# Two query tiles, four result buffers and moved weight splits in a linear-attention and expert kernel

## Chip, cores and metric

The kernel runs on one core of a Trainium2 chip. The metric is the device time of one execution in microseconds (us); three executions of the kernel before gave a median of 298.92 us (298.61 to 301.04).

## The reference

Linear attention with random features over 4 batches, 8 heads, 576 positions (2304 rows of 512 in all), then a top-1 mixture of 8 experts with a capacity per expert.

```python
proj = einsum('bhsd,md->bhsm', x * scale, omega)          # phi: 128 features per head
h = proj - sum(x*x)/2;  phi = exp(h - max(h)) / sqrt(m)   # the max and the square cancel per row
kv = einsum('bhsm,bhsd->bhmd', k_p, v);  z = sum(k_p, axis=2)
x = einsum('bhsm,bhmd->bhsd', q_p, kv) / (einsum('bhsm,bhm->bhs', q_p, z) + 1e-6)
logits = x @ w_gate;  expert_idx = argmax(logits);  gate_w = softmax(logits)[expert_idx]
# per expert, the first `capacity` rows in order are kept
y = relu(x_e @ w1[e]) @ w2[e];  out[i] = gate_w[i] * y[...]   # dropped rows are zero
```

## The kernel before

Every instruction is recorded in the order in which the Python code runs; each engine works through its own list in that order and waits on semaphores. So the order of the code sets the order of the work. Generators in a list `tasks` are advanced by `step(n)` at fixed points of the loops, and `pause(n)` in such a generator lets n of these points pass: that is how side work is spread between the main steps.

The work has three stages, each with its own pool of PSUM banks (`stage(name, pairs, singles)`; a pair is two banks).

- **Key stage** (`psk`: two sum banks, three pairs). Loop `n` over 18 groups of four (batch, head pair, row tile) units: `project` (TensorE, `pjk`), `maxima` (VectorE, `mxk`), `exponent` (ScalarE, eight activations, `exk`), and two groups later the key sums `kv_acc` (TensorE, `ksum`). When half a batch is summed, `kv_out` copies the sums (`kv_sb`, VectorE), GpSimd copies them to `kvc`, TensorE transposes them (`ktr`), VectorE copies (`kvT`), TensorE multiplies by the gate weights (`ksm`), VectorE copies the product into `kv_sb`.
- **Query stage** (`psq`: two pairs, two single banks, two banks `qsum`). Loop `t` over 18 tiles of 128 rows: project tile t (`pjq`), sums of tile t-3 (`numer`, `qsum`), maxima of tile t (`mxq`), results of tile t-3 (`normalise`: `den`, `rec`, `xr`, `lg`, and the write-out to `x_d` on SyncE), transposes of tile t-2 (`transposed`: `qtr`, copies `qpT` on ScalarE), exponentials of tile t (`exq`). The results tile `xr` rotates over three buffers. Side tasks: `route` for three groups of tiles (0 to 4, 5 to 11, 12 to 17) finds each row's expert and its rank and scatters it to a table (GpSimd); `first_item` finds the expert of row 0, loads its weights and splits them in a high and a low part on GpSimd (`split_w_hi`, `split_w_lo`: `w1hi`, `w1lo`, `w2hi`); `first_rows` reads the first item's rows from the table and gathers them (`xg`). Behind the last tiles `transpose_x` transposes the gathered rows and splits them (`xtri`, `xhi` on ScalarE, `xlo` on VectorE).
- **Item stage** (`psi`: four `h` banks, two `y`, two others). Items of 576 rows of one expert: `mm1` makes 16 half steps (8 features blocks f, two halves of rows) of 12 matmuls each (`hi`), `mm2` the second product. In item 0 the last group's rank product (`posr`) and the list of items (`items_list`, `cps`) stand behind the first two half steps. Three items run.

A tile of a new pool waits until the old pool has been read to the end. The rest of the order follows from the functions that the change touches:

## Time and profile before

| | us |
|---|---|
| median of three runs | 298.92 |
| the profiled execution, as timed | 299.85 |
| its span, first to last instruction | 298.1 |
| TensorE busy | 276.0 |
| ScalarE busy | 159.0 |
| VectorE busy | 147.8 |
| GpSimd busy | 79.2 |
| mean granted TensorE clock, share of full speed | 0.983 |

The busy time of TensorE counts matmuls that overlap; what can be gained is where it stands idle, and where its clock is low. The key stage runs to about 50 us, the query stage to 123 us, item 0 to 179 us, items 1 and 2 to 282 us, and then the last results are written.

### The profile page before, as it was taken

How to read it: one execution, taken by the hardware profiler on the slowest of the kernel's cores; microseconds unless marked ns; L12 is line 12 of the kernel's file. 1: busy time of each engine (PE TensorE's matmuls, PEld its weight loads, DVE VectorE, ACT ScalarE, POOL GpSimd, SP SyncE). 2: the span in 40 equal slices, each digit the busy share in tenths (PEclk: the TensorE clock that was granted, in tenths of full speed). 3: DMA queues.
4: the chain of work that ended last, by engine and by line, in shares of the span. 5: the costliest groups of instructions: out<-in, count | busy, mean ns of one | idle time of the engine just before them, and what ended most of it. 6: DMA issues, size and time to landing. Idle time of an engine off the chain costs nothing.

```text
span 298.1 us, 7419 instructions
## 1 busy us (share of the span) xinstructions
PE 276.0 (93%) x2971; PEld 240.0 (81%) x2971; DVE 147.8 (50%) x295; ACT 159.0 (53%) x458; POOL 79.2 (27%) x92
## 2 busy tenths in 40 slices
PE   7999999799999878799999999999999999999940
PEld 5899998688888766799958879996888999778830
DVE  2566664587986796666522332543342152532410
ACT  2998885799899877222243324443531435334210
POOL 1010011003659777035052111700121171011210
PEclk9999999999999999899999999999999999999995
DMA  6998940237991986504869103921811196062120
GB/s 196 388 378 299 318 168 2 55 128 254 373 370 37 360 292 179 178 3 118 274 185 306 38 35 98 315 67 5 297 57 51 37 335 106 0 235 104 43 71 2
DMA packets 30959, 50.37 MB, mean 169 GB/s; under 512 B 5587, under 2 KB 18387, under 8 KB 30900
## 3 DMA queue, kind: packets, MB, share of 16 engines
q1 hardware_dynamic: 27620, 41.46, 41.1%
q0 software_dynamic: 3152, 8.28, 9.2%
q8 instruction: 25, 0.41, 0.6%
q14 instruction: 18, 0.15, 0.2%
q10 hardware_dynamic: 144, 0.07, 0.1%
HBM read 36.80 MB, written 13.28 MB: 168 GB/s over the span
## 4 chain that ended last, share of the span: by engine, by line
PE 73%; DVE 6%; DMA 5%; issue 5%; POOL 4%; SPq 2%; ACT 2%; POOLq 0%; DVEq 0%; ACTq 0%
PE hi L662 9%; PE hi L664 9%; PE hi L663 9%; PE yi L678 7%; PE yi L680 7%; PE yi L679 7%; PE ksum L200 6%; PE pjk L137 5%; PE yi L688 4%; PE qsum L469 3%; PE xtri L323 3%; DMA kraw<-kT 2%; PE pjq L137 2%; PE qtr L460 2%; POOL w1lo L125 2%
## 5 line engine op out<-in xcount | busy, mean ns | idle before, releaser
L662 PE MATMUL hi<-xhi,w1hi 128*128 128x288 f32 x192 | 57.7, 300 | 1.7 <-DVE mxr L349 1.7
L664 PE MATMUL hi<-xlo,w1hi 128*128 128x288 f32 x192 | 57.3, 299 | 0.0
L663 PE MATMUL hi<-xhi,w1lo 128*128 128x288 f32 x192 | 57.2, 298 | 0.0
L667 ACT ACTIVATE hhii<-hi 128x288 fp32r<-128x288 f32 (+1 forms) x48 | 18.5, 385 | 50.0 <-PE hi L664 50.0
L152 ACT ACTIVATE exk<-pjk,mxk 128x128 f32<-128x128 f32 x144 | 38.7, 409 | 8.2 <-DVE mxk L144 8.2
L152 ACT ACTIVATE exq<-pjq,mxq 128x128 f32<-128x128 f32 x144 | 39.5, 403 | 4.8 <-DVE mxq L144 4.8
L670 DVE SCALAR_TENSOR_TENSOR hloi<-hi,hhii 128x288 fp32r<-128x288 f32 (+1 forms) x48 | 20.1, 423 | 39.2 <-ACT hfi L669 27.0
L106 POOL DMA_INDIRECT out<-ysi,idx x15 | 14.6, 975 | 93.9 <-ACT ysi L705 78.3
L678 PE MATMUL yi<-w2hi,hhii 128*128 128x512 f32 x96 | 38.8, 404 | 0.0
L662 PEld LDWEIGHTS hi<-xhi,w1hi 128*128 128x128 f32 x192 | 36.7, 191 | 2.2 <-issue 1.8
L327 DVE TENSOR_TENSOR xlo<-xtri,xhi 128x512 fp32r<-128x512 f32 (+1 forms) x20 | 12.4, 635 | 51.6 <-ACT xhi L326 51.6
L680 PE MATMUL yi<-w2lo,hhii 128*128 128x512 f32 x96 | 37.9, 395 | 0.0
L679 PE MATMUL yi<-w2hi,hloi 128*128 128x512 f32 x96 | 37.9, 395 | 0.0
L663 PEld LDWEIGHTS hi<-xhi,w1lo 128*128 128x128 f32 x192 | 36.7, 191 | 0.0
L664 PEld LDWEIGHTS hi<-xlo,w1hi 128*128 128x128 f32 x192 | 36.6, 191 | 0.0
L705 ACT ACTIVATE ysi<-yi,idx 128x512 f32<-128x512 f32 x12 | 8.3, 688 | 45.9 <-issue 39.2
L144 DVE TENSOR_REDUCE mxk<-pjk 128x8 f32<-128x1024 f32 x18 | 21.9, 1224 | 16.4 <-PE pjk L137 12.1
L311 POOL DMA_INDIRECT xg<-x_d,idx x20 | 22.2, 1110 | 25.5 <-DMA idx<-tab_d 11.7
L469 PE MATMUL qsum<-kv_sb,qpT 128*64 128x73 f32 x576 | 22.4, 229 | 4.3 <-DVE xr L485 3.0
L144 DVE TENSOR_REDUCE mxq<-pjq 128x8 f32<-128x1024 f32 x18 | 21.9, 1216 | 7.8 <-PE pjq L137 7.8
L469 PEld LDWEIGHTS qsum<-kv_sb,qpT 128*64 128x64 f32 x576 | 19.9, 136 | 6.8 <-issue 4.2
L106 POOL DMA_INDIRECT tab_d<-pay,slot x18 | 18.7, 1037 | 22.1 <-DVE ilcnt L592 11.6
(105 smaller groups left out, 425.8 us busy)
## 6 DMA issues: line engine op xcount, KB each, us to landing
w1raw<-w SPq DMA_DIRECT2D x16, 512.0 KB, 7.0
w2raw<-w SPq DMA_DIRECT2D x16, 512.0 KB, 6.4
qraw<-qT SPq DMA_DIRECT2D x6, 768.0 KB, 8.7
x_d<-xr SPq DMA_DIRECT2D x18, 256.0 KB, 5.4
out<-zero_sb SPq DMA_DIRECT2D x6, 768.0 KB, 8.5
v<-va SPq DMA_DIRECT2D x7, 650.0 KB, 7.8
kraw<-kT SPq DMA_DIRECT2D x6, 576.0 KB, 8.5
kraw<-kT SPq DMA_DIRECT2D x3, 192.0 KB, 3.4
```

The costliest lines, as they stand in the source:

```text
L106: ins = nc.gpsimd.indirect_dma_start(out=dst, out_offset=bass.IndirectOffsetOnAxis(ap=index, axis=0), in_=src, in_offset=None, bounds_chec ...
L137: nc.tensor.matmul(pj[:, i, s * M : (s + 1) * M], raw[r, :], om_sb[r, :], start=True, stop=True, skip_group_check=True)
L144: nc.vector.tensor_reduce(mx, pj, op=ALU.max, axis=AX.X, negate=True)
L152: nc.scalar.activation(ex[:, i, s, :], pj[:, i, s, :], AF.Exp, bias=mx[:, i, s : s + 1], scale=1.0)
L311: nc.gpsimd.indirect_dma_start(out=big["xg"][0:n, i, :], out_offset=None, in_=x_d[0:rows, :], in_offset=bass.IndirectOffsetOnAxis(ap=big[" ...
L469: nc.tensor.matmul(qsum[c : c + 64, h // 4, o : o + ROW], qpT[:, h, c : c + 64], kv_sb[(t * 128 + c) // S][:, h, :], start=(h % 4 == 0), s ...
L662: nc.tensor.matmul(pt, whi_[:, k, fs], xhi[:, k, sl], start=(k == 0), stop=False)
L663: nc.tensor.matmul(pt, wlo_[:, k, fs], xhi[:, k, sl], start=False, stop=False)
L664: nc.tensor.matmul(pt, whi_[:, k, fs], xlo[:, k, sl], start=False, stop=(k == 3))
L678: nc.tensor.matmul(pt, hhi[:, f, sl], w2hi, start=(f == 0), stop=False)
L679: nc.tensor.matmul(pt, hlo[:, f, sl], w2hi, start=False, stop=False)
L680: nc.tensor.matmul(pt, hhi[:, f, sl], w2lo, start=False, stop=(f == 7))
```

## The change

The diff without the lines that only follow from it:

```diff
@@ -40,4 +40,4 @@
 
-HI_AT = ({}, {0: ((2, 0),), 1: ((2, 1),), 3: ((2, 2),), 4: ((2, 3),)})
-LO_AT = ({f + 2: ((2, f),) for f in range(4)}, {1: ((2, 0),), 2: ((2, 1),), 5: ((2, 2),), 6: ((2, 3),)})
+HI_AT = ({0: ((2, 0),), 1: ((2, 1),), 3: ((2, 2),), 4: ((2, 3),)}, {0: ((2, 0),), 1: ((2, 1),), 3: ((2, 2),), 4: ((2, 3),)})
+LO_AT = ({2: ((2, 0),), 3: ((2, 1),), 5: ((2, 2),), 6: ((2, 3),)}, {1: ((2, 0),), 2: ((2, 1),), 5: ((2, 2),), 6: ((2, 3),)})
 
@@ -208,4 +208,7 @@
 
-    kvc = const.tile([128, 4 * M], F32, name="kvc")
-    kvT = const.tile([128, 4 * M], F32, name="kvT")
+
+    def row_buffer(name):
+        return small.tile([128, ROW, H], F32, tag="xr", name=name, bufs=4)
+
+    kv_bufs = {}
 
@@ -213,2 +216,5 @@
         yield
+        if g == 0:
+            kv_bufs[b] = row_buffer(f"kvc{b}").rearrange("p c h -> p (c h)")
+        kvc = kv_bufs[b]
         kv = kv_sb[b][:, 4 * g : 4 * g + 4, :]
@@ -223,2 +229,3 @@
             nc.tensor.transpose(tr[:, i * M : (i + 1) * M], kvc[:, i * M : (i + 1) * M], id_sb)
+        kvT = row_buffer(f"kvT{b}").rearrange("p c h -> p (c h)")[:, 0 : 4 * M]
         nc.vector.tensor_copy(kvT, tr)
@@ -329,3 +336,3 @@
 
-    head = {"quiet": True}
+    head = {"routed": 0}
     place = {"ranks": False}
@@ -346,17 +353,4 @@
         sel, p, base, drop, sm = tl(t3, "s"), tl([128, T], "p"), tl([128, T], "b"), tl([128, T], "o"), tl([128, T], "m")
-        head["quiet"] = a == 0
+        gap = 2 if 0 < a and z < NT else 1
         yield from pause(2)
...
         if a == 0:
@@ -366,2 +360,16 @@
             count(bas, a)
+            yield
+        nc.vector.tensor_reduce(mx, lg[:, a:z, :], op=ALU.max, axis=AX.X)
+        yield from pause(gap)
...
@@ -392,14 +400,14 @@
         nc.vector.tensor_reduce(p, sel, op=ALU.add, axis=AX.X)
-        yield
+        yield from pause(gap)
...
         for t in range(a, z):
@@ -407,3 +415,3 @@
             yield from pause(2 if 0 < a and z < NT else 0)
-        head["quiet"] = False
+        head["routed"] += 1
         if z == T0:
@@ -434,13 +442,12 @@
             load_w(2, c, ev)
-
-            while c > 1 and head["quiet"]:
+            yield from pause(2)
+        for c in range(4):
+
+            while head["routed"] < (0, 1, 1, 2)[c]:
                 yield
             split_w_hi(1, c, nc.gpsimd)
-            yield from pause(3 if c < 2 else 1)
+            yield from pause(1 if c else 3)
             for k in range(4):
                 split_w_lo(1, c, nc.gpsimd, k)
-                yield from pause(2 if c < 2 else 1)
-        for c in range(4):
-            split_w_hi(2, c, nc.gpsimd)
-            yield from pause(4)
+                yield from pause(1 if c else 2)
 
@@ -478,3 +485,3 @@
     def normalise(t):
-        xr = small.tile([128, ROW, H], F32, tag="xr", name=f"xr{t}", bufs=3)
+        xr = row_buffer(f"xr{t}")
         av = qsum[:, :, 0 : 4 * ROW].rearrange("p b (h c) -> p c b h", c=ROW)
@@ -501,3 +508,9 @@
     LK = 2
-    ex_l = {}
+    ex_l, exq, qpT_l = {}, {}, {}
+
+    def project_tile(t):
+        c, o = t // QT, t % QT * 128
+        return project([qc[c][:, p, o : o + 128] for p in range(NP)], f"q{t}")
+
+
     for n in range(NK + LK):
@@ -519,2 +532,4 @@
             pj = project_keys()
+        elif n >= NK:
+            pj = project_tile(n - NK)
         step()
@@ -526,2 +541,4 @@
                     load_k(k1 // 2, k1 % 2)
+        else:
+            exq[n - NK] = exponent(pj, maxima(pj, f"q{n - NK}"), f"q{n - NK}")
         step(2)
@@ -529,4 +546,4 @@
             tasks.append(setup())
-        if n in (NK - 4, NK - 2):
-            load_q(0 if n == NK - 4 else 1)
+        if n in (NK - 5, NK - 3):
+            load_q(0 if n == NK - 5 else 1)
     kstack.close()
@@ -539,8 +556,8 @@
 
-    exq, qpT_l = {}, {}
-    for t in range(NT + 3):
+    for t in range(LK, NT + 3):
         if t < NT:
-            c, o = t // QT, t % QT * 128
-            pj = project([qc[c][:, p, o : o + 128] for p in range(NP)], f"q{t}")
-            if t % QT == 0 and c + 2 < NT // QT:
+            pj = project_tile(t)
+        if t == LK or (t < NT and t % QT == 0):
+            c = t // QT
+            if c + 2 < NT // QT:
                 load_q(c + 2)
@@ -567,9 +584,6 @@
             exq[t] = exponent(pj, mx, f"q{t}")
-        else:
-            for i in range(2 * (t - NT), min(2 * (t - NT) + 2, NSUB)):
-                transpose_x(i, "i0")
+        for i in {NT - 1: (0,), NT: (1, 2), NT + 1: (3, 4)}.get(t, ()):
+            transpose_x(i, "i0")
         step(3)
     qstack.close()
-    qps.close()
-    ctx.enter_context(stage("i", 0, 2))
 
@@ -740,4 +754,4 @@
 
-                for _ in chain(*tasks):
-                    pass
+                while tasks:
+                    step()
                 ro = route(*GROUPS[NT - 1])
@@ -749,3 +763,4 @@
                 for half in range(2):
-                    hp = bank(f"h{nm}{f}{half}", "h", 4)
+
+                    hp = pair(f"h{half}")[:, 0, :] if j + f == 0 else bank(f"h{nm}{f}{half}", "h", 4)
                     mm1(f, half, hp, hhi, hlo, hf)
@@ -754,2 +769,4 @@
                 if j == 0 and f == 0:
+                    qps.close()
+                    ctx.enter_context(stage("i", 0, 2))
                     for _ in chain(ro, items_list()):
```

Place by place:

- Key stage: tiles 0 and 1 of the queries are projected in the two extra turns of the key loop (n = 18 and 19), ahead of `ksm` of batch 2 and behind the last key sums, in pairs of the key stage's pool. The query loop starts at t = 2. The first two query loads are issued one turn earlier.
- `xr` has four buffers, and `kvc` and `kvT` use the same four.
- `route` of the middle group takes twice as many points; the count of earlier rows stands at its start.
- `first_item` loads all of w2 first; the w1 splits on GpSimd go on at three places: block 0 at once, 1 and 2 behind the first group's scatters, 3 behind the second's. The high parts of w2 are made on ScalarE in item 0.
- The transposes of the gathered rows start one tile earlier (one, two, two).
- The first two half steps of item 0 use pairs of the query stage; the item stage's pool is opened behind them.

TensorE's list where the key stage passes into the query stage; `ksum` are key sums, `pjq0` the projection of query tile 0, `qtr` transposes, `qsum` the sums of a tile. Before:

```order
L200 MATMUL ksum1_108<-v31_581,exk16_777 64x130 x4
L229 MATMUL ksm2_848<-wg_sb_73,kvT_95 64x16 x8
L200 MATMUL ksum1_108<-v31_581,exk17_815 64x65 x16
L137 MATMUL pjq0_913<-om_sb_67,qraw0_710 128x128 x8
L223 MATMUL ktr3_936<-id_sb_72,kvc_94 128x128 x4
L137 MATMUL pjq1_942<-om_sb_67,qraw0_710 128x128 x8
L229 MATMUL ksm3_951<-wg_sb_73,kvT_95 64x16 x8
L137 MATMUL pjq2_972<-om_sb_67,qraw0_710 128x128 x8
L460 MATMUL qtr00_984<-id_sb_72,exq0_927 128x128 x4
L460 MATMUL qtr02_990<-id_sb_72,exq0_927 128x128 x4
L137 MATMUL pjq3_1005<-om_sb_67,qraw1_786 128x128 x8
L469 MATMUL qsum_912<-kv_sb0_68,qpT0_983 64x73 x16
```

There the projections of tiles 0 to 2 all stand behind the last key sums (`exk17`), with the last batch's `ktr3` and `ksm3` between them. TensorE's list at the same place now:

```order
L200 MATMUL ksum1_106<-v31_582,exk16_782 64x130 x4
L137 MATMUL pjq0_852<-om_sb_67,qraw0_676 128x128 x8
L236 MATMUL ksm2_873<-wg_sb_73,kvT2_832 64x16 x8
L200 MATMUL ksum1_106<-v31_582,exk17_818 64x65 x16
L137 MATMUL pjq1_899<-om_sb_67,qraw0_676 128x128 x8
L137 MATMUL pjq2_958<-om_sb_67,qraw0_676 128x128 x8
L467 MATMUL qtr00_973<-id_sb_72,exq0_864 128x128 x4
L467 MATMUL qtr02_979<-id_sb_72,exq0_864 128x128 x4
L229 MATMUL ktr3_994<-id_sb_72,kvc3_834 128x128 x4
L137 MATMUL pjq3_1001<-om_sb_67,qraw1_752 128x128 x8
L476 MATMUL qsum_957<-kv_sb0_68,qpT0_972 64x73 x16
L236 MATMUL ksm3_1028<-wg_sb_73,kvT3_999 64x16 x8
```

Two projections moved up between the key sums, and `ktr3` and `ksm3` of the last batch moved down behind the first transposes and the first sums.

VectorE's list around the results of tiles 11 and 12, where the routing of tiles 5 to 11 begins (`mxr5`, `dr5`, `vr5`, `vm`, `oh`, and the count `cum`). Before:

```order
L485 TENSOR_TENSOR xr11_1773<-qsum_912,rec11_1776 128x584
L489 TENSOR_REDUCE lg_81<-xr11_1773 128x8
L349 TENSOR_REDUCE mxr5_1781<-lg_81 128x7
L351 TENSOR_TENSOR dr5_1782<-lg_81,mxr5_1781 128x56
L353 SCALAR_TENSOR_TENSOR vr5_1784<-dr5_1782,desc_sb_77 128x56
L358 TENSOR_REDUCE vm_84<-vr5_1784 128x7
L360 TENSOR_TENSOR oh_82<-vr5_1784,vm_84 128x56
L144 TENSOR_REDUCE mxq15_1844<-pjq15_1816 128x8
L482 TENSOR_SCALAR den12_1847<-qsum_912 128x8
L484 RECIPROCAL rec12_1849<-den12_1847 128x8
L485 TENSOR_TENSOR xr12_1846<-qsum_912,rec12_1849 128x584
L335 TENSOR_REDUCE cum_83<-oh_82 128x8
```

There five routing steps stand in one piece ahead of the maxima of tile 15. VectorE's list at the same place now:

```order
L496 TENSOR_REDUCE lg_81<-xr11_1770 128x8
L342 TENSOR_REDUCE cum_83<-oh_82 128x8
L362 TENSOR_REDUCE mxr5_1778<-lg_81 128x7
L364 TENSOR_TENSOR dr5_1779<-lg_81,mxr5_1778 128x56
L144 TENSOR_REDUCE mxq15_1838<-pjq15_1811 128x8
L489 TENSOR_SCALAR den12_1841<-qsum_957 128x8
L491 RECIPROCAL rec12_1843<-den12_1841 128x8
L492 TENSOR_TENSOR xr12_1840<-qsum_957,rec12_1843 128x584
L366 SCALAR_TENSOR_TENSOR vr5_1781<-dr5_1779,desc_sb_77 128x56
L496 TENSOR_REDUCE lg_81<-xr12_1840 128x8
L371 TENSOR_REDUCE vm_84<-vr5_1781 128x7
L373 TENSOR_TENSOR oh_82<-vr5_1781,vm_84 128x56
```

The routing steps stood in one piece between `lg` of tile 11 and the maxima of tile 15; now the later three stand behind the results of tile 12, and the count stands ahead.

TensorE's list at the end of the query stage, behind the sums of tile 15; `xtri` are the transposes of the gathered rows. Before:

```order
L460 MATMUL qtr160_2051<-id_sb_72,exq16_1937 128x128 x4
L460 MATMUL qtr162_2057<-id_sb_72,exq16_1937 128x128 x4
L323 MATMUL xtri00_2063<-id_sb_72,xg_905 128x128 x4
L323 MATMUL xtri01_2070<-id_sb_72,xg_905 128x128 x4
L469 MATMUL qsum_912<-kv_sb3_71,qpT16_2050 64x73 x16
L460 MATMUL qtr170_2105<-id_sb_72,exq17_2004 128x128 x4
L460 MATMUL qtr172_2111<-id_sb_72,exq17_2004 128x128 x4
L323 MATMUL xtri02_2117<-id_sb_72,xg_905 128x128 x4
L323 MATMUL xtri03_2124<-id_sb_72,xg_905 128x128 x4
L469 MATMUL qsum_912<-kv_sb3_71,qpT17_2104 64x73 x16
L323 MATMUL xtri04_2155<-id_sb_72,xg_905 128x64 x4
L662 MATMUL hi000_2192<-xhi_906,w1hi0_883 128x288
```

There the last transpose of the gathered rows stands between the last tile's sums and the first half step. TensorE's list at the same place now:

```order
L476 MATMUL qsum_957<-kv_sb3_71,qpT15_1981 64x73 x16
L467 MATMUL qtr160_2046<-id_sb_72,exq16_1932 128x128 x4
L467 MATMUL qtr162_2052<-id_sb_72,exq16_1932 128x128 x4
L330 MATMUL xtri01_2058<-id_sb_72,xg_950 128x128 x4
L330 MATMUL xtri02_2065<-id_sb_72,xg_950 128x128 x4
L476 MATMUL qsum_957<-kv_sb3_71,qpT16_2045 64x73 x16
L467 MATMUL qtr170_2109<-id_sb_72,exq17_1994 128x128 x4
L467 MATMUL qtr172_2115<-id_sb_72,exq17_1994 128x128 x4
L330 MATMUL xtri03_2121<-id_sb_72,xg_950 128x128 x4
L330 MATMUL xtri04_2128<-id_sb_72,xg_950 128x64 x4
L476 MATMUL qsum_957<-kv_sb3_71,qpT17_2108 64x73 x16
L676 MATMUL h0_2190<-xhi_951,w1hi0_928 128x288
```

The transposes of the gathered rows moved one tile up, and the sums of the last tile now stand directly ahead of the first half step, which is in a bank of the query stage (`h0`).

## Rows read from the trace of the kernel before

**Rows 1.** Busy time by stretch. Columns: the stretch, its length, the busy time (and instructions) of TensorE, its weight loads, VectorE, ScalarE and GpSimd, the granted TensorE clock as a share of full speed, the DMA share and GB/s.

```profile
46.90:58.20 11.30, 8.92 (x162) 7.68 (x162) 6.29 (x10) 6.63 (x26) 0.80 (x2) 1.00 0.04 6
...
106.00:123.16 17.16, 13.84 (x235) 11.88 (x232) 12.88 (x36) 11.69 (x32) 10.03 (x11) 1.00 0.57 183
...
123.16:150.90 27.74, 27.74 (x202) 27.32 (x204) 16.58 (x57) 6.84 (x23) 8.63 (x8) 0.94 0.48 150
```

**Rows 2.** Instructions in order of time, all engines, where the key stage passes into the query stage. Columns: start, duration, engine, line, operation, output and input, shapes, count; in brackets the idle time of the engine before it and what ended it.

```profile
49.01 1.13 PE L200 MATMUL ksum<-v,exk 128*64 128x65 f32 x32
...
50.67 1.16 PE L137 MATMUL pjq<-om_sb,qraw 64*128 64x128 f32 x16 [0.53 <-DVE kv_sb L215]
...
51.77 0.66 PE L223 MATMUL ktr<-id_sb,kvc 128*128 128x128 f32 x4
...
51.94 1.22 DVE L144 TENSOR_REDUCE mxq<-pjq 128x8 f32<-128x1024 f32 x1 [1.32 <-PE pjq L137]
...
53.20 2.18 ACT L152 ACTIVATE exq<-pjq,mxq 128x128 f32<-128x128 f32 x8 [3.88 <-DVE mxq L144]
...
53.81 0.65 PE L229 MATMUL ksm<-wg_sb,kvT 128*64 128x16 f32 x16 [0.30 <-DVE kvT L224]
...
55.43 1.16 PE L137 MATMUL pjq<-om_sb,qraw 64*128 64x128 f32 x16 [0.97 <-ACT exq L152]
...
57.98 1.12 ACT L461 COPY qpT<-qtr 128x512 f32<-128x512 f32 x2
...
58.19 1.16 PE L137 MATMUL pjq<-om_sb,qraw 64*128 64x128 f32 x16 [0.58 <-ACT exq L152]
...
59.28 1.25 PE L469 MATMUL qsum<-kv_sb,qpT 128*64 128x73 f32 x32
...
59.45 1.22 DVE L144 TENSOR_REDUCE mxq<-pjq 128x8 f32<-128x1024 f32 x1 [1.60 <-PE pjq L137]
...
61.02 0.77 DVE L485 TENSOR_TENSOR xr<-qsum,rec 128x584 f32<-128x584 f32 x1
...
64.78 1.16 PE L137 MATMUL pjq<-om_sb,qraw 64*128 64x128 f32 x16
```

**Rows 3.** Instructions in order of time, TensorE, in the query stage and at the start of item 0: those ahead of which it idles.

```profile
79.77 1.25 PE L469 MATMUL qsum<-kv_sb,qpT 128*64 128x73 f32 x32 [0.66 <-DVE xr L485]
...
93.41 1.25 PE L469 MATMUL qsum<-kv_sb,qpT 128*64 128x73 f32 x32 [0.28 <-DVE xr L485]
...
101.14 1.25 PE L469 MATMUL qsum<-kv_sb,qpT 128*64 128x73 f32 x32 [1.08 <-DVE xr L485]
...
105.75 1.25 PE L469 MATMUL qsum<-kv_sb,qpT 128*64 128x73 f32 x32 [1.25 <-DVE cum L335]
...
112.53 1.25 PE L469 MATMUL qsum<-kv_sb,qpT 128*64 128x73 f32 x32 [1.01 <-DVE xr L485]
...
115.09 1.15 PE L323 MATMUL xtri<-id_sb,xg 128*128 128x128 f32 x8 [0.29 <-ACT qpT L461]
...
118.72 1.15 PE L323 MATMUL xtri<-id_sb,xg 128*128 128x128 f32 x8 [0.29 <-ACT qpT L461]
...
123.16 0.37 PE L662 MATMUL hi<-xhi,w1hi 128*128 128x288 f32 x1 [1.72 <-DVE mxr L349]
```

**Rows 4.** Instructions in order of time, VectorE: the subtraction of the three routing groups, and a results tile.

```profile
75.50 1.00 DVE L351 TENSOR_TENSOR dr<-lg,mxr 128x40 f32<-128x40 f32 x1
...
100.23 0.77 DVE L485 TENSOR_TENSOR xr<-qsum,rec 128x584 f32<-128x584 f32 x1 [1.80 <-DMA x_d<-xr]
...
101.53 1.08 DVE L351 TENSOR_TENSOR dr<-lg,mxr 128x56 f32<-128x56 f32 x1
...
123.16 0.21 DVE L351 TENSOR_TENSOR dr<-lg,mxr 128x48 f32<-128x48 f32 x1
```

**Rows 5.** Instructions in order of time, GpSimd: weight splits and scatters.

```profile
72.65 2.79 POOL L125 TENSOR_TENSOR w1lo<-w1raw,w1hi 128x256 fp32r<-128x256 f32 x4
...
75.41 1.04 POOL L122 TENSOR_SCALAR w1hi<-w1raw 128x1024 fp32r<-128x1024 f32 x1
...
101.47 1.07 POOL L122 TENSOR_SCALAR w2hi<-w2raw 128x1024 fp32r<-128x1024 f32 x1
...
111.81 1.00 POOL L106 DMA_INDIRECT tab_d<-pay,slot  x1 [0.30 <-issue]
...
113.12 0.97 POOL L106 DMA_INDIRECT tab_d<-pay,slot  x1 [0.30 <-issue]
```

**Rows 6.** Instructions in order of time, ScalarE: the exponentials of tile 17.

```profile
112.13 2.19 ACT L152 ACTIVATE exq<-pjq,mxq 128x128 f32<-128x128 f32 x8
```

**Rows 7.** Instructions in order of time, TensorE, VectorE and ScalarE, behind the first two half steps of item 0: the rank product, VectorE's read of the second half step, and the Relus of the first halves of two feature blocks that follow each other.

```profile
127.95 0.20 PE L374 MATMUL posr<-oh,tri_b 128*128 128x48 bf16 x1
...
128.65 0.39 DVE L670 SCALAR_TENSOR_TENSOR hloi<-hi,hhii 128x224 fp32r<-128x224 f32 x1 [2.18 <-ACT hfi L669]
...
130.04 0.41 ACT L667 ACTIVATE hhii<-hi 128x288 fp32r<-128x288 f32 x1 [1.43 <-PE hi L664]
...
133.23 0.41 ACT L667 ACTIVATE hhii<-hi 128x288 fp32r<-128x288 f32 x1 [1.12 <-PE hi L664]
```

**Rows 8.** Busy time by stretch as in rows 1, two stretches of 2 us at the start of item 0.

```profile
124.00:126.00 2.00, 2.00 (x12) 2.00 (x11) 0.65 (x3) 0.41 (x1) 0.00 (x0) 0.57 1.03 384
126.00:128.00 2.00, 2.00 (x12) 1.93 (x12) 0.46 (x1) 0.00 (x0) 0.00 (x0) 0.58 0.08 23
```

More of the change, by code (lines that the diff above doesn't have):

```diff
@@ L366, in route @@
             count(bas, a)
+            yield
+        nc.vector.tensor_reduce(mx, lg[:, a:z, :], op=ALU.max, axis=AX.X)
+        yield from pause(gap)
+        nc.vector.tensor_tensor(d, lg[:, a:z, :], mx.unsqueeze(2).to_broadcast(t3), op=ALU.subtract)
+        yield from pause(gap)
+        nc.vector.scalar_tensor_tensor(
+            val, d, 0.0, desc_sb.unsqueeze(1).to_broadcast(t3), op0=ALU.is_ge, op1=ALU.mult
+        )
+        nc.scalar.activation(ex, d, AF.Exp)
+        yield from pause(gap)
+        nc.vector.tensor_reduce(vm[:, a:z], val, op=ALU.max, axis=AX.X)
+        yield from pause(gap)
+        nc.vector.tensor_tensor(oh[:, a:z, :], val, vm[:, a:z].unsqueeze(2).to_broadcast(t3), op=ALU.is_equal)
+        yield from pause(gap)
         while not place["ranks"]:
@@ L392, in route @@
         nc.vector.tensor_reduce(p, sel, op=ALU.add, axis=AX.X)
-        yield
+        yield from pause(gap)
         nc.vector.tensor_scalar(drop, p, cap_f, BIG, op0=ALU.is_ge, op1=ALU.mult)
         nc.vector.scalar_tensor_tensor(base, vm[:, a:z], -float(REG), p, op0=ALU.mult, op1=ALU.add)
-        yield
+        yield from pause(gap)
         nc.vector.scalar_tensor_tensor(slot[:, a:z], drop, float(E * REG), base, op0=ALU.add, op1=ALU.add)
-        yield
+        yield from pause(gap)
         nc.vector.tensor_reduce(sm, ex, op=ALU.add, axis=AX.X)
-        yield
+        yield from pause(gap)
         nc.vector.tensor_scalar(sm, sm, 1e-9, None, op0=ALU.add)
-        yield
+        yield from pause(gap)
         nc.vector.reciprocal(pay[:, a:z, 1].bitcast(F32), sm)
-        yield
+        yield from pause(gap)
         for t in range(a, z):
```

12 lines of the change are left out of this document (removed).

## The prediction

> **What bounds the kernel now.** I read the stretches first, then the instructions in order of time where TensorE idles. TensorE is the bound nearly everywhere: outside the entry and the end of the query stage it idles only where a result is late. The table by stretch shows three places that the change touches [rows 1]. The entry into the query stage has TensorE busy 8.92 of 11.30 us, the end of that stage 13.84 of 17.16 us, and the first half of item 0 has no idle time but a clock of 0.94. In between, single waits of 0.66 to 1.25 us stand on TensorE's row [rows 3]. All times below are of the profiled execution (span 298.1 us, 299.85 us as timed); that is 0.9 us above the median of 298.92, and I carry the difference in us to the median.
>
> **1. The entry: two projections moved forward.** Before, the key sums end at 49.01 + 1.13 = 50.1. The projection of tile 0 starts at 50.67, its maximum at 51.94, its exponentials at 53.20, and the projection of tile 2 waits for the latter (0.97 us), that of tile 3 for the exponentials of tile 1 (0.58 us) [rows 2]. The change puts the projections of tiles 0 and 1 ahead of and behind the last key sums. This starts the chain earlier: exponentials of tile 0 from about 51.2. But these two tiles now lie in the banks of the key stage's pool, and the first tile of the query stage's pool waits for the whole old pool, as [rows 2] show: the projection at 50.67 waits 0.53 us for VectorE's last copy out of a key sum's bank, though it writes another bank. The last reader of the old pool now is the set of eight exponentials of tile 1. Step by step: last key sums end at 50.1 + 1.1 (one projection, 50.67 to 51.77) = 51.2; tile 1 projected by 52.3; its maximum from 52.5 (0.17 later, as 51.77 to 51.94) to 53.7; its exponentials, 2.18, to 56.0. Only then comes tile 2. TensorE idles 52.3 to 56.0, 3.7 us in one piece, where it had 2.4 in four pieces.
>
> From there: tile 2 projected 57.1, first transposes (about 1.0) 58.1; the transposes of the last batch's sums, which used to fill a gap, wait for the first copy of a transposed half (half of 1.12) and end at 58.9; tile 3 projected 60.0; first sums (about 1.2) 61.2; the gate product of the last batch (about 0.5) 61.7. Its copy on VectorE stands ahead of the maximum of tile 3, so this maximum starts at 62.0 instead of 60.2. From the start of a maximum to the end of the results tile takes 61.02 + 0.77 - 59.45 = 2.34, so the results are there at 64.35; TensorE, ready for the next sums at 63.8, waits 0.6. Then 1.2 + 1.0 to the projection of tile 5: 66.6. Before it is at 64.78 [rows 2]. **Cost +1.85 us.** The bounds: -1.9 (the exponentials start 2 us earlier and nothing else is in the way) to +2.3.
>
> **2. The clock at the entry.** [...] The stretch at half clock cost 1.6 us: 24 matmuls took 127.95 - 123.16 = 4.79, where the next 24 take 133.23 - 130.04 = 3.19 [rows 7]. [...] **Cost +1.3 us**, bounds 0 and 1.6. [...]
>
> **3. The body of the query stage.** Four buffers instead of three for the results: the two waits of VectorE for a buffer that is still being written out (the longer is 1.80 us at 100.23 [rows 4]) go, since the buffer of four tiles ago left one tile earlier. They stand behind TensorE's waits of 0.28 and 1.08 us. The wait of 1.25 us behind them is VectorE's lateness passed on: the late results, then a block of routing steps in one piece, one of which (the subtraction) took 1.08 us instead of 0.21 [rows 3, 4]. Both long subtractions end with a split of GpSimd that started beside them (75.41 + 1.04, 101.47 + 1.07), and the one with GpSimd idle took 0.21 [rows 4, 5]. The change takes both splits away from these places: the second w1 split waits for the first scatter, the w2 splits go to ScalarE. So the wait of 0.66 us behind the first block goes too, and spreading the second block over two tiles takes the rest. **Gain 0.66 + 0.28 + 1.08 + 1.25 = 3.27 us**; bounds 1.9 (if the 1.25 stays as 0.9 and the 0.66 only halves) and 3.3.
>
> [...]
>
> **4. The end of the stage.** Waits of 1.01, 0.29, 0.29 and 1.72 us [rows 3], 3.3 in all. The 1.72 is the new pool waiting for the last split of x; the first two half steps now use old query banks and need no new pool. But the transposes of x, drawn one tile forward, take a bank that ScalarE empties late: the copy of x behind the first transpose stands behind the eight exponentials of tile 17 (2.19), and the second half of tile 16's transposes stands behind that (copies of 0.56 each) [rows 2, 6]. By the same stepping as above this makes one wait of 1.5 us, and about 0.4 in small ones. **Gain 3.3 - 1.9 = 1.4 us**; bounds 0.7 and 2.5. The first item then starts at about 120.4.
>
> **5. Behind the first two half steps.** The pool is now opened here, so the rank product waits until VectorE has read the second half step's bank: before, the product stands at 127.95 right behind the matmuls, and that read ends at 128.65 + 0.39 [rows 7]. **Cost +1.1 us**, bounds 0.7 and 1.9 (with the collision of 3). And with the 1.72 us wait goes the half clock of [rows 8]: **gain 1.6 us**, 0 if the waits of 1.5 and 1.1 us bring it down as well.
>
> **Nothing for the rest.** Four casts of w2 (about 1 us each, as GpSimd's) join ScalarE in item 0, where it works 1.0 of every 3.19 us between Relus, with four banks of slack; without that slack, 1 us each. The last w1 split ends at about 127 and is needed at the seventh feature step, near 140; were it late, TensorE would wait by as much. SyncE issues two w2 loads earlier, ahead of two result copies, which the fourth buffer covers.
>
> **Sum.** +1.85 + 1.3 - 3.27 - 1.4 + 1.1 - 1.6 = -2.0 us: 298.92 - 2.0 = 296.9.
>
> **Rivals.**
> - The clock stays up at the entry (the drop of [rows 8] came after transposes and several waits, not after one). Then -3.3: 295.6. Chance 0.27.
> - The early projection works: tile 2 is not held for tile 1's exponentials, and the entry gains 1.9 where I lose 1.85 + 1.3. Then 291.9. Against it stands the wait at 50.67 for a bank it does not use. Chance 0.08.
> - Half clock at the end as well: the 1.5 us wait lies between 1.25 (no drop) and 1.72 (drop). Another 1.4: 298.3. Chance 0.15.
> - Slower than before: half clock at the entry does not heal within a tile, because at half clock the chain from projection to exponentials keeps TensorE waiting. A tile takes (64.78 - 58.19) / 2 = 3.3 us, 6.6 at half clock; from 0.6 of a further tile on the gain of 2.0 is eaten, with one it is 300.2, with two 303.5. For it: ScalarE is nearly as full as TensorE there. Against: the drop of [rows 8] healed by itself. Chance 0.08.
> - The forecast: 0.42.
>
> **How the numbers follow.** About 1% (3 us) is what a measurement of this kernel can tell from no change. Faster by more than that means below 295.9: the early projection (0.08), two thirds of the case with the clock up (0.18) and a quarter of the forecast's own spread (0.10) give 0.36. Slower by over 1% (above 301.9) needs two tiles at half clock or several bounds at once: 0.06. The rest, 0.58, is within 1%. The range leaves out 0.08 at the bottom and about 0.08 at the top: from 295.6 less the open bounds of the entry and the end (1.8), 293.8, to 298.3 with the collision of 0.8 and some room, 299.4.
>
> **What would show it.** Entry: one wait of about 3.7 us ahead of the third projection, put down to ScalarE's exponentials, and a lower clock around 56 to 60; its absence breaks step 1 or 2. Body: no result tile waits for its buffer, both subtractions at 0.2 us, the four waits gone. End: a wait of about 1.5 us inside tile 16's transposes; first half step at about 120.4 (plus the clock's 1.3). Item 0: a wait of about 1.1 us ahead of the rank product, put down to VectorE's read of the half step, and clock 1.00 behind it. I am wrong if the entry costs nothing, or if half clock shows in more places than the entry.

## The result and the profile after

The changed kernel takes 302.14 us (median of 20 runs; 300.56 to 304.26), the kernel before 299.68 in 20 runs beside it: ratio 1.0082, 95% interval 1.0063 to 1.0101. It is slower by 2.5 us, where 2.0 us less was forecast; the time lies outside the range. The profiled execution of the changed kernel spans 300.3 us (before 298.1) at a mean clock of 0.977 (before 0.983). Each trace is one execution: over its 20 runs the mean clock of the changed kernel goes from 0.970 to 0.982, with 0.976 in the middle; over 21 later runs the kernel before has 0.971 to 0.989, with 0.982 in the middle.

The difference by places, each from the start of the named instruction in the two traces:

| place | before | after | later by | this stretch | forecast |
|---|---|---|---|---|---|
| projection of tile 5 | 64.78 | 68.15 | +3.37 | +3.37 | +3.15 |
| projection of tile 17 | 108.15 | 108.55 | +0.40 | -2.97 | -3.27 |
| first half step | 123.16 | 122.36 | -0.80 | -1.20 | -1.4 |
| first Relu of the fourth feature block | 136.63 | 138.10 | +1.47 | +2.27 | -0.5 |
| first Relu of item 1 | 181.00 | 182.56 | +1.56 | +0.09 | 0 |
| end of the span | 298.1 | 300.3 | +2.2 | +0.6 | 0 |

The first three stretches came out nearly as worked out; the fourth has the other sign. (In the runs of the next section, but for two, every version took some 11 us more, the kernel before among them: 310.8 to 312.1 us.)

The entry, which answers to [rows 2]: the changed kernel's TensorE in order of time, idle time in brackets.

```profile
56.19 1.16 PE L137 MATMUL pjq<-om_sb,qraw 64*128 64x128 f32 x16 [3.58 <-ACT exq L152]
57.28 1.76 PE L467 MATMUL qtr<-id_sb,exq 128*128 128x128 f32 x8
59.01 1.09 PE L229 MATMUL ktr<-id_sb,kvc 128*128 128x128 f32 x4
60.03 1.59 PE L137 MATMUL pjq<-om_sb,qraw 64*128 64x128 f32 x16
...
65.95 1.25 PE L476 MATMUL qsum<-kv_sb,qpT 128*64 128x73 f32 x32 [0.62 <-DVE xr L492]
...
68.15 1.16 PE L137 MATMUL pjq<-om_sb,qraw 64*128 64x128 f32 x16
```

There is one wait of 3.58 us ahead of the third projection, put down to the exponentials. Behind it `qtr`, `ktr` and `pjq3` take up to 1.7 times as long as elsewhere: for part of this stretch the granted clock is half of full speed (0.50 from 58 to 60.5 us; the mean from 54 to 64 us is 0.83), called half clock below. In the stretches of [rows 8] the kernel before has it too: 1.00 up to 124.25, and 0.50 in each quarter of a us from 124.5 to 127.5. The rank product behind the first two half steps, which answers to [rows 7]:

```profile
128.12 0.18 PE L382 MATMUL posr<-oh,tri_b 128*128 128x48 bf16 x1 [2.32 <-DVE hloi L684]
```

VectorE and GpSimd of the changed kernel just ahead of it; the last routing group, which answers to [rows 4, 5]:

```profile
124.31 0.21 DVE L364 TENSOR_TENSOR dr<-lg,mxr 128x48 f32<-128x48 f32 x1
124.56 1.59 DVE L366 SCALAR_TENSOR_TENSOR vr<-dr,desc_sb 128x48 f32<-128x48 f32 x1
...
126.42 0.54 DVE L373 TENSOR_TENSOR oh<-vr,vm 128x48 bf16<-128x48 f32 x1
...
127.32 0.75 DVE L684 SCALAR_TENSOR_TENSOR hloi<-h,hhii 128x288 fp32r<-128x288 f32 x2
```

```profile
125.01 1.08 POOL L122 TENSOR_SCALAR w1hi<-w1raw 128x1024 fp32r<-128x1024 f32 x1
126.17 2.79 POOL L125 TENSOR_TENSOR w1lo<-w1raw,w1hi 128x256 fp32r<-128x256 f32 x4
```

The split of the fourth w1 block meets the routing group (the collision, below): two steps together take 2.13 us instead of 0.4, the read of the half step's bank (`hloi`) comes that much later, and the rank product waits 2.32 us for it instead of 1.1. Busy time by stretch in the changed kernel (columns as in [rows 8]; the clock is the third number from the end):

```profile
128.00:130.00 2.00, 1.88 (x18) 1.87 (x18) 1.42 (x10) 0.00 (x0) 0.96 (x2) 0.81 0.05 17
130.00:132.00 2.00, 2.00 (x10) 2.00 (x10) 1.72 (x16) 0.41 (x1) 1.41 (x2) 0.50 0.01 0
132.00:134.00 2.00, 2.00 (x15) 2.00 (x14) 1.76 (x11) 0.68 (x3) 1.58 (x2) 0.84 0.02 1
```

The half clock did not go with the wait that it stood behind: it moved behind the new one. The same view around the first half steps shows 1.00 until 128. The first Relu of the fourth feature block, before and after:

```profile
136.63 0.41 ACT L667 ACTIVATE hhii<-hi 128x288 fp32r<-128x288 f32 x1 [1.35 <-PE hi L664]
```

```profile
138.10 0.41 ACT L681 ACTIVATE hhii<-hi 128x288 fp32r<-128x288 f32 x1 [1.13 <-PE hi L678]
```

### The profile page after: what moved, and what is told of

It reads as the page before. It is cut to its first block, busy times and chain, and to the rows that moved or that the text cites. A ratio compares the mean times of both kernels' runs of the same rounds, so it can differ in the third digit from the quotient of the medians.

```text
span 300.3 us, 7418 instructions
## 1 busy us (share of the span) xinstructions
PE 278.3 (93%) x2971; PEld 241.8 (81%) x2971; DVE 147.7 (49%) x295; ACT 162.1 (54%) x462; POOL 73.8 (25%) x88
## 4 chain that ended last, share of the span: by engine, by line
PE 64%; DVE 5%; DMA 4%; issue 2%; ACT 2%; POOL 0%; DVEq 0%; ACTq 0%
PE hi L676 8%; PE hi L678 8%; PE hi L677 8%; PE yi L692 7%; PE yi L693 7%; PE yi L694 7%; DMA x_d<-xr 4%; PE qsum L476 4%; PE yi L702 4%; PE pjq L137 3%; PE qtr L467 3%; PE xtri L330 3%; DVE xr L492 2%; ACT exq L152 1%; DVE mxq L144 1%
## 5 line engine op out<-in xcount | busy, mean ns | idle before, releaser
L676 PE MATMUL hi<-xhi,w1hi 128*128 128x288 f32 x184 | 55.2, 300 | 0.0
L678 PE MATMUL hi<-xlo,w1hi 128*128 128x288 f32 x184 | 54.9, 299 | 0.0
L677 PE MATMUL hi<-xhi,w1lo 128*128 128x288 f32 x184 | 54.9, 299 | 0.0
L681 ACT ACTIVATE hhii<-hi 128x288 fp32r<-128x288 f32 (+1 forms) x46 | 17.7, 384 | 46.1 <-PE hi L678 46.1
L678 PEld LDWEIGHTS hi<-xlo,w1hi 128*128 128x128 f32 x184 | 35.3, 192 | 0.0
L676 PEld LDWEIGHTS hi<-xhi,w1hi 128*128 128x128 f32 x184 | 35.1, 191 | 0.1
L677 PEld LDWEIGHTS hi<-xhi,w1lo 128*128 128x128 f32 x184 | 35.2, 191 | 0.0
L468 ACT COPY qpT<-qtr 128x512 f32<-128x512 f32 x36 | 19.6, 591 | 9.9 <-PE qtr L467 6.8
L137 PE MATMUL pjq<-om_sb,qraw 64*128 64x128 f32 x288 | 21.3, 288 | 3.6 <-ACT exq L152 3.6
L200 PE MATMUL ksum<-v,exk 128*64 128x65 f32 (+1 forms) x576 | 23.4, 232 | 0.2 <-ACT exk L152 0.2
```

The lines of the kernel that those rows point to most:

```text
L137: nc.tensor.matmul(pj[:, i, s * M : (s + 1) * M], raw[r, :], om_sb[r, :], start=True, stop=True, skip_group_check=True)
L200: nc.tensor.matmul(acc[c : c + 64, i * 2 * VW + o : i * 2 * VW + o + (z - a) * VW], ex[:, i, c : c + 64], v[:, i, a * VW : z * VW], start= ...
L468: nc.scalar.copy(qpT[:, 2 * p : 2 * p + 4, :], tr.rearrange("p (h t) -> p h t", h=4))
L676: nc.tensor.matmul(pt, whi_[:, k, fs], xhi[:, k, sl], start=(k == 0), stop=False)
L677: nc.tensor.matmul(pt, wlo_[:, k, fs], xhi[:, k, sl], start=False, stop=False)
L678: nc.tensor.matmul(pt, whi_[:, k, fs], xlo[:, k, sl], start=False, stop=(k == 3))
```

## The experiments

Ratios are to the kernel before in the same group of runs.

**The changed kernel again**, as the control. 

> The changed kernel itself, beside the next three on one chip. On the chips of the runs so far the kernel before took 311 to 312 us instead of 299.7, so a ratio of a variant to it says little of its ratio to the changed kernel. If the same holds for the changed kernel, its ratio is 1.008 as measured first; if the slower chips lengthen other places in it, it is above 1.008 and their places show as waits that the first profiles don't have.

The ratio is 1.014 (1.006 to 1.022). Its row at the rank product:

```profile
142.57 0.18 PE L382 MATMUL posr<-oh,tri_b 128*128 128x48 bf16 x1 [0.99 <-DVE hloi L684]
```

```profile
142.00:144.00 2.00, 1.43 (x17) 1.43 (x17) 1.36 (x7) 1.02 (x2) 0.00 (x0) 1.00 0.02 6
144.00:146.00 2.00, 2.00 (x17) 2.00 (x16) 1.69 (x16) 0.41 (x1) 1.06 (x1) 1.00 0.00 0
```

In this trace TensorE stands still for 5.62 us while GpSimd sends the second group's scatters (such stalls are shown below for the kernel before). GpSimd has finished its split by 136.3, before the first step of the last routing group that could meet it, at 138.80; `vr` takes 0.21, the wait is 0.99, and the clock behind it stays at 1.00. So the same program without the collision has about the wait that step 5 worked out, and no half clock behind it.

**The entry.** First the early projection is undone in the changed kernel:

```diff
-        elif n >= NK:
-            pj = project_tile(n - NK)
...
-    for t in range(LK, NT + 3):
+    for t in range(NT + 3):
...
```

> The changed kernel with its first part alone undone: the projections of tiles 0 and 1 stand behind the last key sums again, and the query loads one turn later. My theory (the two early tiles hold the whole old pool, and the wait they make brings the clock down) expects what the traces show as the difference at the projection of tile 5, 68.15 against 64.78, so 3.4 us less than the changed kernel: about 298.8 us beside its 302.1, no wait over 1 us and clock 1.00 between 50 and 64 us. The rival (the loss lies behind the query stage, and the delay of the entry is taken back by waits that the body has anyway) expects under 1 us, about 301.5.

The ratio is 1.011 (1.007 to 1.015), against 1.014 for the control of another group: the intervals are too wide to tell. On its trace the projection of tile 5 starts at 64.41, no wait between 50 and 64 us is over 0.96 us and the clock is 1.00. Then the early projection alone in the kernel before, in a group where that took 299.9 us:

> The kernel before with the early projection of the first two query tiles alone (and the query loads one turn earlier). My theory (the whole old pool holds the third projection, and the clock falls in the wait) expects a wait of 3.6 us ahead of the third projection, half clock behind it and the projection of tile 5 3.4 us later; the waits of the body do not depend on it, so 2.5 to 3.4 us more than the kernel before. The rival (the stalls during the scatters, which come at times that GpSimd sets, take the delay back) expects under 1 us more.

It takes 303.94 against 299.91 us, ratio 1.0106 (1.0068 to 1.0144): 3.2 us more by the ratio, 4.0 by the medians. The rival falls. TensorE of its trace:

```profile
55.95 2.08 PE L137 MATMUL pjq<-om_sb,qraw 64*128 64x128 f32 x16 [3.59 <-ACT exq L152]
...
69.14 1.16 PE L137 MATMUL pjq<-om_sb,qraw 64*128 64x128 f32 x16
...
128.87 0.37 PE L671 MATMUL hi<-xhi,w1hi 128*128 128x288 f32 x1 [1.73 <-DVE mxr L349]
```

```profile
130.00:132.00 2.00, 2.00 (x17) 2.00 (x16) 0.82 (x3) 0.41 (x1) 0.00 (x0) 1.00 0.90 333
```

The wait is there, but that the time came so near the 3.37 of the table is partly chance. Here half clock lasts longer (0.66 from 54 to 64 us), the projection of tile 5 is 4.4 us later than in [rows 2], and a wait of 2.54 us at 106.97, again with half clock, makes that 5.9 us at tile 17; on the other side, the wait of 1.73 us ahead of the first half step has no half clock behind it, though that of 1.72 in [rows 3] has. In the next run the two waits of the changed kernel are filled with work (14 idle projections, 16 idle matmuls):

```diff
+    for i in range(14):
+        nc.tensor.matmul(fill[:, i % 2, 0:M], qc[0][0:D, 0, 0:128], om_sb[0:D, :], ...)
     kstack.close()
...
```

> The changed kernel with 14 extra projections of no use in the wait at the entry (0.23 us each by the trace of the run with 46 of them, so 3.2 us) and 16 extra matmuls of 288 columns ahead of the rank product (2.1 us); their results are dropped. What follows starts no earlier. My theory (the waits bring the clock down) expects clock 1.00 throughout: 1.2 us less at the entry and 1.9 less in item 0, so 3 us less than the changed kernel. The rival (the clock falls for another reason, or the time at half clock is hidden) expects the time of the changed kernel.

The ratio is 1.013 (1.002 to 1.024), no difference from the control that can be measured, where 3 us were expected; the second filling has no half clock to remove, since the control has none there. Its entry on the trace:

```profile
52.31 3.29 PE L551 MATMUL fill<-om_sb,qraw 64*128 64x128 f32 x28
56.07 1.16 PE L137 MATMUL pjq<-om_sb,qraw 64*128 64x128 f32 x16 [0.47 <-ACT exq L152]
57.16 1.09 PE L467 MATMUL qtr<-id_sb,exq 128*128 128x128 f32 x8
```

The clock is 1.00 from 54 to 64 us, and from the third projection to that of tile 5 it takes 10.82 us (56.07 to 66.89), where the changed kernel takes 11.96: the half clock at the entry costs 1.1 us and comes with the idle time. All six traces with the wait of 3.58 or 3.59 us have half clock behind it, the two with the wait filled have none. (A run with 46 fills, which took 10.43 us and so 6.9 too long, measured only itself: ratio 1.037.)

**The release of the pool.** Here two pairs of the key stage lie in a pool of their own, which stays open to the items:

```diff
+        third = ring["pairs"] == 3 and ring["n"] % 3 == 1
+        pool, tag, n = (ring["pool"], "third", 1) if third else (ppool, "pj", 2)
...
```

> The changed kernel with two pairs of the key stage in a pool of their own that lives until the items (a tile in it waits for the tile before it in its own banks alone), and the third pair, with tile 0, and the key sums in a pool that closes with the key stage. My theory (the release of the whole pool holds the third projection) expects it right behind the second, at about 52.5, no wait over 3 us, clock 1.00, then the first transposes at 54.1 behind the last copy out of a key sum, the projection of tile 3 near 57.2 and that of tile 5 near 64.9 instead of 68.15: 3.2 us less than the changed kernel. The rival (ScalarE, which must do both tiles' exponentials first, holds everything) expects tile 5 no earlier than 67, so about 1 us less.

The ratio is 1.009 (1.005 to 1.013), 0.9 us less than the control by the medians, which their intervals do not tell from nothing, where 3.2 were expected. Its TensorE:

```profile
51.84 2.06 PE L144 MATMUL pjq<-om_sb,qraw 64*128 64x128 f32 x32
54.81 1.06 PE L474 MATMUL qtr<-id_sb,exq 128*128 128x128 f32 x8 [0.92 <-DVE kv_sb L228]
57.15 0.63 PE L236 MATMUL ktr<-id_sb,kvc 128*128 128x128 f32 x4 [1.28 <-ACT qpT L475]
57.71 1.16 PE L144 MATMUL pjq<-om_sb,qraw 64*128 64x128 f32 x16
```

Projections 1 and 2 stand in one piece, the 3.58 us are gone, and the projection of tile 5 is at 65.40. So the release of the whole pool makes the long wait, as step 1 says; the gain that the time should show from it was not seen. The next two runs also have the fourth w1 block split on ScalarE and VectorE; the second of them has the old entry:

> The kernel with two key pools and the fourth w1 block split off GpSimd: the changed kernel without its two faults. My theory expects 3.2 us at the entry, 1.3 less wait ahead of the rank product and up to 1.9 of half clock behind it: 4.5 to 6.4 us less than the changed kernel, and 2.0 to 3.9 less than the kernel before. The rival (each gain is taken back by waits behind it) expects no more than 1 us less than the changed kernel.

> The changed kernel with the old entry (projections behind the last key sums) and the fourth w1 block split off GpSimd. My theory: 3.4 us from the entry, 1.3 from the rank product's wait and up to 1.9 from the half clock, 4.7 to 6.6 us less than the changed kernel; with the same two gains in the last kernel, the early projection in itself is worth nothing (0 to 0.3 us). The rival (the early projection helps once the pool is out of its way) expects this one 2 us slower than the last.

The ratios are 1.0067 (1.0029 to 1.0105) and 1.0061 (1.0042 to 1.0080): 2.3 and 2.4 us less than the control by the medians, half of the 4.5 that were expected at least. With its fault removed, the early projection brings nothing that can be measured: ScalarE's copies, behind its exponentials, still hold the transposes (1.28 us above), and in the first of these two half clock came at the entry as well (0.83 from 54 to 64 us). One pool for the whole kernel, in which the two half steps of a feature block share a tile of two banks, was no way out:

> The changed kernel with one pool of PSUM banks for all three stages: the two key sums and the tile's sums share two banks, the third pair of the key stage (with tile 0) becomes the banks of the transposes, and a feature block's two half steps take one pair. No tile waits for a whole pool. My theory (the pool's release is what makes both new waits) expects no wait over 1 us between 50 and 60 us, the projection of tile 5 at 63 or before (68.15 in the changed kernel), no wait ahead of the rank product and clock 1.00 at the entry: 5 us less there and 2.3 to 4.2 less behind the first half steps, so 293 to 295 us where the changed kernel has 302.1. The rival (the exponentials of the two early tiles hold the third projection anyway, through ScalarE) expects the entry as it is in the changed kernel, and the gain at the second place alone, about 299.

It takes 384.91 us, ratio 1.22 (382.91 with the w1 split moved as well). Its longest waits (engine, what it waited for, total, times, longest):

```profile
PE hi L674 <- DVE hloi L682: 26.5, 24, 3.6
PE third L467 <- ACT qpT L468: 17.1, 17, 3.1
```

24 waits of TensorE ahead of a half step end with VectorE's read of an earlier one. In the edit the two half steps of a block are one tile, which may be why; no run takes this by itself.

**The collision.** Here the split of the fourth w1 block is taken off GpSimd:

```diff
-        for c in range(4):
+        for c in range(3):
...
+                    split_w_hi(1, 3)
+                    split_w_lo(1, 3)
                     next(pre, 0)
```

> The changed kernel with the split of the fourth w1 block on ScalarE and VectorE right behind the list of items, ahead of the next item's loads, so that GpSimd is idle while the last routing group is worked on. My theory: the routing step that took 1.59 us takes about 0.2, the one behind it 0.2 instead of 0.54, and the wait ahead of the rank product is 0.8 to 1.0 instead of 2.32 us: 1.4 us less than the changed kernel, and 1.9 more if the half clock behind it goes with it. The rival (the long step has nothing to do with GpSimd) expects no change.

The ratio is 1.014 (1.005 to 1.022); `vr` takes 0.21, the wait is 0.99, and the clock behind it is 1.00. As the control shows the same, this run does not decide. (A first form, with the split in the third and fifth feature blocks of item 0, has a ratio of 1.048, 1.040 to 1.055: there ScalarE waits 10.07 us for the load of that block, and TensorE 9.08 us behind it at 165.83.) What speaks is all 20 traces together (60 routing groups): each routing step of over 0.45 us, 18 in all, has a weight split of GpSimd beside it. 17 of them end within 0.1 us behind the end of a split; the other, the `dr` at 102.59 in the changed kernel, ends 0.09 us behind that of a gather. The reverse does not hold: 71 other routing steps overlap a split and stay below 0.45, all 40 reductions among them.

**The parts behind the entry, each in the kernel before.** First stands the kernel before itself:

> The kernel before itself, for its profile beside the next three. If the 11 us that it is longer on these chips come from one cause that all versions share, its trace shows the same long stalls as the changed kernel there: about 3 us with the first group's scatters, 2 us near 110 and 5 to 7 us with the second group's. If the moved splits or the spread routing cause them, it does not show them.

Its rows with the second group's scatters, all engines:

```profile
116.40 0.97 POOL L106 DMA_INDIRECT tab_d<-pay,slot  x1 [0.31 <-issue]
...
121.51 0.97 POOL L106 DMA_INDIRECT tab_d<-pay,slot  x1 [0.31 <-issue]
123.74 0.17 DVE L482 TENSOR_SCALAR den<-qsum 128x8 f32<-128x8 f32 x1 [7.83 <-remote]
123.86 1.07 ACT L461 COPY qpT<-qtr 128x512 f32<-128x512 f32 x2 [5.42 <-remote]
...
124.49 1.97 PE L323 MATMUL xtri<-id_sb,xg 128*128 128x128 f32 x8 [6.32 <-ACT qpT L461]
```

While GpSimd sends seven scatters, the other engines stand still for 5 to 8 us; the kernel before has this stall too, so the change does not make it. Then the body alone:

> The kernel before with the third part alone: four buffers for the results, the routing spread, and the weight splits at their new places; entry and end as before. My theory (the four waits of 0.66, 0.28, 1.08 and 1.25 us go) expects 3.0 us less than the kernel before, the gain that the changed kernel's trace shows between the projections of tiles 5 and 17. The rival (on these chips the scatters set the pace of the stage, and waits only change their place) expects the time of the kernel before, within 1 us.

The ratio is 1.0013 (0.9967 to 1.0059): no gain. The kernel with the old entry (above) has the same body, and its trace tells where it goes. From the last key maximum to the maximum of tile 15 it takes 57.7 us, the kernel before in this group 60.8: 3.1 ahead, as expected. To that of tile 17 it takes 68.7 against 67.4: 1.3 behind. In the kernel before, splits stand between the five gathers; here four gathers follow each other (103.50 to 108.20), and ahead of the sums at 109.92 TensorE idles 2.43 us. Here the rival holds; in the first trace, which has no such stalls, the gain is kept (2.97). Next come buffers and routing without the splits' new places:

> The kernel before with four buffers and the spread routing, the weight splits where they were. My theory: the waits of 0.28 and 1.08 and most of the 1.25 go, the 0.66 stays, since the split beside the first routing group is still there: 2.0 to 2.6 us less than the kernel before. The rival (the splits beside the routing are what counts) expects 0.5 to 1 us less.

The ratio is 1.018 (1.011 to 1.026), slower, where 2.0 to 2.6 us less was expected; on its trace the routing step `vr` takes 2.50 us beside two w2 splits. Next the end alone:

```diff
+        for i in {NT - 1: (0,), NT: (1, 2), NT + 1: (3, 4)}.get(t, ()):
...
-    qps.close()
-    ctx.enter_context(stage("i", 0, 2))
...
+                    hp = pair(f"h{half}")[:, 0, :] if j + f == 0 else bank(f"h{nm}{f}{half}", "h", 4)
...
```

> The kernel before with the end alone: transposes of the gathered rows one tile earlier, the first two half steps in banks of the query stage and the new pool opened behind them. By the changed kernel's trace the end gains 1.2 us up to the first half step and loses 2.9 behind it where the last w1 split collides with the last routing group; in the kernel before that split is done earlier, so a wait of 1.0 us is left ahead of the rank product and the half clock at the first item either stays (0.5 us more than the kernel before at most) or goes (1.5 us less). The rival (the late pool costs more than it gives, with or without that split) expects 1.5 us more or above.

It takes 309.11 against 311.40 us, ratio 0.9952 (0.9924 to 0.9980), the one part that gains. The same two views as for the control:

```profile
137.19 0.18 PE L374 MATMUL posr<-oh,tri_b 128*128 128x48 bf16 x1 [0.99 <-DVE hloi L667]
```

```profile
138.00:140.00 2.00, 2.00 (x17) 2.00 (x16) 1.73 (x15) 0.41 (x1) 0.65 (x1) 1.00 0.00 0
140.00:142.00 2.00, 2.00 (x18) 2.00 (x17) 1.72 (x10) 0.47 (x2) 1.39 (x3) 1.00 0.01 0
```

Where the kernel before has 0.57 and 0.58 behind its first half step in the same group, the clock here is 1.00. Next, the pool's place in the changed kernel is undone:

> The changed kernel with the item stage's pool opened ahead of the first half steps again, as before. My theory: the first half step then waits for the last results tile (ends at 123.68 on VectorE), so it starts at 123.7 instead of 122.36, but the 2.3 us wait ahead of the rank product goes. The second feature block starts at 127.0, or at 128.6 if the half clock comes behind the first wait; in the changed kernel it starts at 128.33 and loses 1.9 more to the half clock. So 1.7 to 3.3 us less: 298.8 to 300.4. The rival (opening the pool later pays for itself by the wait of 1.4 us that it takes away) expects 0.8 to 1.4 us more: 303 or above.

The ratio is 1.018 (1.014 to 1.023): slower than the control if anything. The first half step waits 1.40 us for the results tile, as worked out, and the half clock, there since the stall, lasts through it to about 145. Last come the buffers alone on top of the end, in the group at 299.9 us:

> The kernel before with the end and with four buffers for the results (kvc and kvT among them); routing and splits where they were. My theory: on top of the 2.3 us that the end alone gave, the waits of 0.28 and 1.08 us for a result's buffer go, and nothing moves on GpSimd: 1.0 to 1.4 us less than the end alone, a ratio to the kernel before of 0.991 to 0.992. The rival (the wait for a buffer falls into a stall with the gathers anyway) expects the ratio of the end alone, 0.995.

It takes 302.59 us, ratio 1.0079 (1.0048 to 1.0110), slower. VectorE, GpSimd and TensorE of this kernel:

```profile
109.28 2.69 DVE L407 TENSOR_SCALAR mr<-mr 128x7 f32<-128x7 f32 x1
```

```profile
109.89 2.05 POOL L122 TENSOR_SCALAR w2hi<-w2raw 128x1024 fp32r<-128x1024 f32 x2
```

```profile
114.66 2.21 PE L475 MATMUL qsum<-kv_sb,qpT 128*64 128x73 f32 x32 [2.51 <-DVE xr L491]
```

Earlier results bring a routing step of 0.2 us beside two w2 splits; it ends with them, the next results are late, TensorE waits 2.51 us, and the sums behind the wait take 2.21 instead of 1.25: half clock. With the splits left where they were, end and buffers together do not pay. (This trace also has half clock at the entry, 0.83 from 54 to 64 us, which the edit does not touch.)

This kernel has the end of the changed kernel, no long stalls and no split beside the last routing group; only its w2 splits stay on GpSimd. So it shows about what step 5 is without the collision:

```profile
125.29 0.40 PE L665 MATMUL h<-xhi,w1hi 128*128 128x288 f32 x1
...
127.38 0.21 DVE L359 SCALAR_TENSOR_TENSOR vr<-dr,desc_sb 128x48 f32<-128x48 f32 x1
...
129.72 0.18 PE L380 MATMUL posr<-oh,tri_b 128*128 128x48 bf16 x1 [0.99 <-DVE hloi L673]
...
138.17 0.41 ACT L670 ACTIVATE hhii<-hi 128x288 fp32r<-128x288 f32 x1 [1.13 <-PE hi L667]
```

```profile
130.00:132.00 2.00, 2.00 (x18) 2.00 (x16) 1.68 (x11) 0.19 (x1) 0.12 (x1) 1.00 0.13 47
132.00:134.00 2.00, 2.00 (x18) 2.00 (x17) 1.73 (x15) 0.69 (x3) 1.70 (x2) 1.00 0.01 0
```

From the first half step to the first Relu of the fourth block it takes 12.88 us, the kernel before 13.47, the changed kernel 15.74. That is 0.6 us less than before, as step 5 forecast (0.5), and 2.9 us less than with the collision.

## Why the prediction was wrong

**Right** (forecast in brackets). Steps 1 and 2 together cost 3.37 us (3.15). The wait is 3.58 (3.7), with the cause named there, and the later wait 0.62 (0.6); the half clock is 1.1 of it (1.3), which leaves 2.3 for step 1 (1.85, at most 2.3). No run shows the 1.3 that the sum takes for the clock at the entry; the runs showed 1.1 in its place, with the clock at 1.00 through the wait and 0.50 to 0.54 from 57.5 to 61 us. Step 3 gained 2.97 us (3.27); a result still waits 1.10 for a buffer and the second `dr` takes 0.50. In step 4 the waits inside the end are 1.10 and 0.24 to 0.30, the gain 1.2 (1.4). That step put the wait of 1.72 us down to the last split of x, where its row in [rows 3] names `mxr`, which stands behind that split on VectorE; the gain does not hang on it. Of the rivals, "clock stays up", "early projection works" and "does not heal" fell.

**Wrong: step 5, which has the collision in its bound and not in its sum.** The collision that step 5 and the range name is that of the last w1 split with the last routing group; the split ran at 125.01 to 128.96. No run shows one of 0.8 us there, about what the first group's subtraction took beside a split (1.00) over the 0.21 of the last [rows 4, 5]. In its place two steps took 1.39 and 0.33 us longer, which made the wait ahead of the rank product 2.32 instead of 0.99. Behind that longer wait the half clock came back: from the rank product to the first Relu of the fourth block it takes 9.98 us (128.12 to 138.10), before 8.68 (127.95 to 136.63). This is the prediction's own sign of being wrong, half clock in more places than the entry. Behind a wait of 0.98 or 0.99 us there, no half clock followed in nine traces. So this one term is worth 1.3 for the wait and 1.3 for the clock, of the 2.8 us that step 5 is off. With both the sum is +0.6 instead of -2.0; the traces have +2.2, of which 0.6 is in the tail, which the forecast has at 0 (0.4 of it behind the last instruction of GpSimd, where the results are written out), and 1.0 is small misses of all steps. That the collision made the wait is shown; that the wait made the half clock rests on one trace with a wait of 2.32 us. No run has the changed kernel without the collision and without the long stalls, so the gain of removing it was not measured.

**What spoke for the collision.** [rows 4, 5] show such steps beside a split before the change, and step 3 reads them there; in the changed kernel `vr` took 1.59 us beside the split, and 0.21 in the control without. Those rows should have set the term.

**The risk.** The half clock was given to the end in one rival (0.15), by the wait inside it of 1.5 us; the wait behind it was in no rival, though its bound of 1.9 lay above the 1.72 that had half clock behind it before. That rival took the lengths of 1.25 and 1.72 us as if they divided the waits without half clock from those with it; the 1.73 of the entry alone passed at clock 1.00, so they do not. The slower case was looked for at the entry alone.

**Open.** It stays open why all engines stall with the scatters in some runs and not in others of the same program; a group with these stalls (before: 311.2 us) and one without (299.9) ran on the same chip. Whether the end alone gains without the stalls was not tried. The kernel with the end alone is the only one whose interval lies below 1.

## What to carry to other kernels

A new pool's first tile waits for the last reader of the whole old pool (3.58 us here), so a step that is moved ahead of the change of pools can hold everything behind it: find the last reader before moving. A short step on VectorE's way to TensorE can be held to the end of the GpSimd split beside it (1.59 us instead of 0.21 here), so each shift in time, even a gain, must be stepped against the other engine's list; what is seen there belongs in the sum. And price a wait with the clock: those of 1.72, 2.32 and 3.58 us in the first two traces cost their length and 1.1 to 1.6 us behind it, though one of 1.73 in another trace cost its length alone.

## What the runs showed of the hardware

A VectorE step with one tensor as its input is held too: `mr`, a tensor_scalar of 128x7, took 2.69 us beside two splits, and 0.17 in the kernel before. Long steps can begin up to 0.6 us before the split and still end with it (109.28 against 109.89; `vr` in the changed kernel 124.56 against 125.01). Half clock also came at the entry behind waits of which the longest was 0.97 us, in two of eight traces with the old entry (clock 0.83 from 54 to 64 us in them, 1.00 in the others), and the same wait of 1.72 or 1.73 us ahead of the first half step had it behind it in two traces and not in a third; so the length of one wait does not decide it alone. And TensorE, VectorE and ScalarE stood still for 5 to 8 us while GpSimd sent a run of seven scatters, in some runs of a program and not in others.
